# Window attention and routed experts on one core: grouped one-hots, split first loads, and weights loaded at other steps

## The chip, the core and the metric

The kernel runs on one NeuronCore of a Trainium2 chip. A core has five engines that run side by side, each taking its own instructions in order: TensorE (PE in the profile; PEld is its loading of weights, which overlaps the multiplying), VectorE (DVE), ScalarE (ACT), GpSimd (POOL) and SyncE (SP, which here only issues transfers). SBUF is the working memory of 128 partitions, PSUM the eight banks into which PE writes its products. Transfers between DRAM and SBUF run on 16 DMA engines that all issuing engines share.

The metric is the time of one execution in microseconds of the device, lower is better. The kernel before took 696.98 us, the median of three runs (695.01, 696.98, 697.22).

## The reference, cut to what matters

Two blocks follow each other. The first is attention of 8 batches x 8 heads over 576 positions of width 64, where a position sees itself and the 63 before it. Its output, regarded as 4608 tokens of width 512, goes through a layer of eight experts of which each token uses one.

```python
scores = scale * np.matmul(q, k.transpose(0, 1, 3, 2))
mask = (rel >= 0) & (rel < 64)              # rel = query position - key position
scores = np.where(mask, scores, -1e9)
attn = np.exp(scores - scores.max(-1, keepdims=True))
attn = attn / (attn.sum(-1, keepdims=True) + 1e-9)
x = np.matmul(attn, v)                      # then (B, H, S, D) -> (4608, 512)

logits = x @ w_gate                         # 8 experts
expert_idx = np.argmax(logits, axis=1)
gate_w = ...                                # the softmax probability of that expert
h = np.maximum(x_of_expert @ w1[e], 0.0)    # w1[e]: 512 x 1024
y_of_expert = h @ w2[e]                     # w2[e]: 1024 x 512
out = gate_w[:, None] * y                   # each row back in its token's place
```

All numbers are float32.

## The kernel before

**Attention.** A *unit* is two batches (a group, `BG = 2`) and two heads (a head pair, `g`); there are 16 units. Each has nine tiles of 128 queries, taken three at a time: a *step*, 48 in all. Eight tiles come from the first 512 positions of the two batches, the ninth from their last 64 positions (the *ends*, "rests" in the code, which are loaded for all eight heads of a group at once by `load_rests`).

The order of instructions is written out by hand: `step(s)` emits for several steps at once what keeps PE busy. In one call PE gets, in this order, `scored(s+1)` (scores, L700), `weighted(s-1)` (attention times v, L746), at the end of a unit the logits of its three steps (L783), `flipped(s)` (transposes of the exponentials, L731, copied to SBUF at L733), `turned(s+3)` (transposes of q and k that step s+3 needs, L665 and L657, copied at L670 and L660) and `x_turned(s-2)` (L771). DVE masks scores and takes their extremes (`masked`, L713) and divides by the sums (L756 to L760); ACT takes the exponentials (L723). Two banks hold scores, so the scores of a step wait for the masking of the step before. The calls begin at s = -3, so that `turned(0)` comes first; the call for s = -2 leaves its `turned` out, and the call for s = -1 makes up for it, after `scored(0)`.

Loads for later units are issued at the first step of a unit, on SP: the ends if a new group is near, then v two units ahead, then q and k three units ahead (`load_qk`, L614). v is kept in two forms. `load_v` loads the first (L637), and POOL copies it shifted by 64 positions into the second (L638, L642, L646), directly behind the issue. So POOL's later work stands in its queue behind the landing of that v.

Other work hangs in `todo[s]`, a list that is emitted at the end of step s: the loading of the first expert's w1 (four pieces on ACT's queue at steps 1, 2, 4 and 5), the four sums of its quarters on POOL (`left_sums`, steps 9 to 12), the routing of a finished group (`choose`), and the weighting of its rows by the gate with their storing in `x_dram` (`weigh` on POOL, L886; `store`).

**Routing and the table of slots.** Tokens of an expert get consecutive places, in tiles of 256 tokens. The table `perm_i` that says which token sits in which slot is made by matmuls: the slot's number splits into a high part (the column) and a low part (the partition). `lo` holds a one-hot of the low part, `hi` one of the high part, and a token's number is brought in as two bf16 factors, `toks`, so that it stays exact. Before, `lo` holds both planes, each already multiplied by one of the factors, made by `place(j)` one column of tokens after the other (two DVE instructions per column, L875), and the table is the sum of 72 matmuls (L927). A first, small table for expert 0's first two tiles is made before the last group is routed (`first_tiles`, L982 and L990, 54 matmuls).

**Experts.** A product of a whole tile is seven quarter products (Strassen's scheme in Winograd's form): `hidden` makes seven products with w1's quarters and their sums (L353), `output` seven with w2's (L397). `tile0` and `tile1` are expert 0's first two tiles. Both are generators: each `next` emits one product and what belongs to it, so that other work can be put between. `tile0` is emitted between pieces of the last group's routing and of `slot_table`. Tokens of the following tile are fetched from `x_dram` by `gather` (POOL, L285), and turned by 16 block transposes on DVE (`turned_blocks`, L324); in `tile1` all 16 stand in `output`, behind the sums of h (L142), and in front of ACT's copies (`keep_turned`, L336). The tile behind is a half tile (L453). `load_w1(1)` and `load_w2(1)` (L159, L162) are emitted on SP after `tile1`; their memory is the attention's, so they wait until the table's matmuls have read `hi`.

**Start.** POOL makes the mask by eleven selections over pieces of it (L587 to L590), DVE clears four columns of `lo` (L998), and PE runs eight matmuls on them while the first q and k are under way (L1000). The ends of group 0 are issued directly behind unit 0's q and k.

The few lines that place the work around the change:

```python
if s + 3 < N and s != -2:
    if s == -1:
        turned(1)
    turned(s + 3)
...
xsp = held.enter_context(tc.tile_pool(name="xsp", bufs=7))
...
tile1 = chain(hidden(0), output(0, blocks))
```

## Time and profile before

| | before |
|---|---|
| median of three runs | 696.98 us |
| the profiled execution's own time | 692.44 us |
| its span, first to last instruction | 690.7 us |
| granted TensorE clock | 0.997 |
| busy: PE, PEld | 671.8 us (97%), 590.5 us (85%) |
| busy: DVE, ACT, POOL | 500.6, 262.2, 357.0 us |
| moved by DMA | 94.51 MB in 135742 packets |
| packets under 512 bytes | 114543 |

The page counts an engine as busy while one of its instructions runs. Matmuls are pipelined and their ends are modelled, so short waits of PE are read better from PEld, whose records follow each other at a fixed distance while PE is supplied. In a row of the timeline stand the start in us, the busy us, engine, line, operation, what is written from what, the form and the number of instructions; a bracket at its end gives the engine's idle time before the row and what ended it. The name of a releaser is inferred, and can be wrong where several waits end together. The stages are: attention to about 189 us, `tile0` with the last routing and the table to 232, `tile1` to 257, and then the tiles of all experts.

### The profile page before, as it was taken

Reading aid. Unit: us, or ns where it says so; the run is one execution under the profiler, and the core shown is the slowest. Engines: PE = TensorE matmul, PEld = TensorE weight load, DVE = VectorE, ACT = ScalarE, POOL = GpSimd, SP = SyncE. Lnnn points to the kernel's source line nnn. Section 1 sums busy time; section 2 is a strip of 40 time slices with the busy share of each in tenths; the row PEclk is TensorE's granted clock in tenths of the full one; section 3 lists DMA queues with packets and bytes.
Section 4 is the critical chain, followed back from the end, with each engine's and each line's share of the span. In section 5 each row is a group of like instructions: output and inputs, shape, how many; then the busy total and the mean of one; then the engine's idle time right before and its main releaser. Section 6 shows DMA issues by size and latency. Waiting matters only on the chain. (4 is left out here: it accounts for less than half of the span.)

```text
span 690.7 us, 17952 instructions
## 1 busy us (share of the span) xinstructions
PE 671.8 (97%) x6902; PEld 590.5 (85%) x6902; DVE 500.6 (72%) x1650; ACT 262.2 (38%) x660; POOL 357.0 (52%) x364
## 2 busy tenths in 40 slices
PE   7999999999999999999999999999899999999996
PEld 5888888888788987998899899899599799689995
DVE  5767898898959578775686586577767586866864
ACT  4989888889845011211121121111121121121211
POOL 7316578577771218676451446446265756264012
PEclk9999999999999999999999999999999999999998
DMA  9999888877524442723601171270145171211012
GB/s 216 251 210 199 192 206 244 202 199 198 162 78 168 155 157 77 268 69 128 230 1 64 61 262 44 70 269 32 65 156 190 51 256 51 65 39 63 2 63 61
DMA packets 135742, 94.51 MB, mean 137 GB/s; under 512 B 114543, under 2 KB 114559, under 8 KB 135616
## 3 DMA queue, kind: packets, MB, share of 16 engines
q1 hardware_dynamic: 113952, 38.28, 22.4%
q0 software_dynamic: 8544, 26.50, 11.9%
q10 hardware_dynamic: 13120, 28.05, 11.3%
q8 instruction: 78, 1.28, 0.7%
q14 instruction: 48, 0.39, 0.2%
HBM read 73.94 MB, written 20.45 MB: 137 GB/s over the span
## 5 line engine op out<-in xcount | busy, mean ns | idle before, releaser
L324 DVE STREAM_TRANSPOSE v_m<-qk_m 32x256 f32<-32x256 f32 x320 | 139.3, 435 | 6.8 <-DMA qk_m<-x_dram,at_g 0.8
L285 POOL DMA_INDIRECT qk_m<-x_dram,at_g x42 | 45.1, 1075 | 164.2 <-DVE v_m L324 154.1
L353 PE MATMUL bank<-qk_m,s 128*128 128x128 f32 x1024 | 122.5, 275 | 0.0
L353 PEld LDWEIGHTS bank<-qk_m,s 128*128 128x128 f32 x1024 | 118.3, 192 | 0.0
L723 ACT ACTIVATE pr<-pr,mx 128x128 f32<-128x128 f32 x288 | 89.6, 391 | 22.2 <-DVE mx L713 21.7
L353 PE MATMUL bank<-qk_m,w 128*128 128x128 f32 x768 | 94.2, 276 | 1.0 <-PEq L1166 0.6
L353 PEld LDWEIGHTS bank<-qk_m,w 128*128 128x128 f32 x768 | 90.3, 192 | 4.6 <-issue 4.3
L713 DVE CUSTOM_DVE_ANT_0 pr<-bank,mask 128x128 f32<-128x128 f32 x288 | 64.4, 286 | 15.8 <-PE bank L700 14.6
L304 POOL DMA_INDIRECT out_dram<-v_m,at_s x42 | 42.5, 1011 | 56.9 <-DVE v_m L393 52.7
L393 DVE TENSOR_TENSOR v_m<-bank,v_m 128x256 f32<-128x256 f32 (+1 forms) x95 | 43.8, 480 | 38.1 <-PE bank L397 27.3
L142 POOL TENSOR_TENSOR s<-w 128x1024 f32<-128x1024 f32 x22 | 52.2, 2374 | 0.0
L638 POOL COPY v_m<-v_m 64x520 f32<-64x520 f32 x32 | 19.8, 618 | 62.1 <-DMA v_m<-in_v_dram 52.8
L397 PE MATMUL bank<-qkT_m,v_m 128*128 128x256 f32 x216 | 48.3, 379 | 0.0
L746 PEld LDWEIGHTS bank<-v_m,pT 128*64 128x64 f32 x1152 | 40.4, 137 | 9.0 <-issue 3.4
L746 PE MATMUL bank<-v_m,pT 128*64 128x65 f32 x1152 | 47.4, 227 | 0.1
L360 ACT COPY qk_m<-bank 128x512 f32<-128x512 f32 x16 | 9.4, 587 | 99.9 <-PE bank L353 73.7
L336 ACT COPY qk_m<-v_m 128x512 f32<-128x512 f32 x40 | 22.7, 615 | 61.4 <-DVE v_m L324 61.4
L397 PEld LDWEIGHTS bank<-qkT_m,v_m 128*128 128x128 f32 x216 | 41.0, 190 | 5.5
L700 PE MATMUL bank<-qkT_m 64*64 64x128 f32 x1152 | 43.1, 278 | 1.6 <-DVE qkT_m L670 1.6
L886 POOL TENSOR_SCALAR xs<-xs,gate 128x512 f32<-128x512 f32 x27 | 42.2, 1574 | 0.9 <-DVE gate L846 0.3
L731 PE MATMUL bank<-ident,pr 128*128 128x128 f32 x288 | 42.0, 282 | 0.0
L363 DVE TENSOR_TENSOR qk_m<-bank,qk_m 128x512 f32<-128x512 f32 x16 | 11.1, 692 | 40.7 <-PE bank L353 40.7
(202 smaller groups left out, 1249.2 us busy)
## 6 DMA issues: line engine op xcount, KB each, us to landing
w<-in_moe_w_dram ACTq DMA_DIRECT2D x9, 2048.0 KB, 8.1
qk_m<-in_q_dram SPq DMA_DIRECT2D x32, 256.0 KB, 5.1
v_m<-in_v_dram SPq DMA_DIRECT2D x64, 128.0 KB, 4.3
qk_m<-in_k_dram SPq DMA_DIRECT2D x30, 256.0 KB, 5.1
qk_m<-in_moe_w_dram ACTq DMA_DIRECT2D x3, 2048.0 KB, 10.6
w<-in_moe_w_dram SPq DMA_DIRECT2D x2, 2048.0 KB, 14.2
w<-in_moe_w_dram ACTq DMA_DIRECT2D x4, 512.0 KB, 5.8
x_dram<-xs POOLq DMA_DIRECT2D x4, 512.0 KB, 5.6
```

The lines of the kernel that those rows point to most:

```text
L142: op()
L285: G.indirect_dma_start(out=xg[c], out_offset=None, in_=x_dram[:, :], in_offset=bass.IndirectOffsetOnAxis(ap=at_g[:, c : c + 1], axis=0),)
L304: put = G.indirect_dma_start(out=out[:, :], out_offset=bass.IndirectOffsetOnAxis(ap=at_s[:, c : c + 1], axis=0), in_=ys[c], in_offset=None ...
L324: V.transpose(out=xn[b * QD : (b + 1) * QD, :, :, a * QD : (a + 1) * QD].rearrange("p c g i -> p (c g) i"), in_=rows[a * QD : (a + 1) * QD ...
L353: nc.tensor.matmul(acc[:, f, :], lhsT=a[:, g, f * P : (f + 1) * P], rhs=b[:, g, :], start=(first and f == 0 and g == 0), stop=(g == HG - 1 ...
L393: plus = lambda out, a, b: V.tensor_tensor(out=out, in0=a, in1=b, op=ALU.add)
L397: nc.tensor.matmul(acc, lhsT=a[:, f, :], rhs=b[:, f, :], start=(start and f == 0), stop=(stop and f == HF - 1), skip_group_check=True,)
L700: nc.tensor.matmul(out_, lhsT=qT[rows, t, a * WINDOW : (a + 1) * WINDOW], rhs=rhs, start=True, stop=True, skip_group_check=True,)
L713: V.tensor_tensor_reduce(out=prs[h][:, m, :], in0=scs[h][:, m, :], in1=mask[:, m0 + m, :], scale=-scale, scalar=-2 * MASKED, op0=ALU.add, ...
L723: nc.scalar.activation(out=y, in_=y, func=AF.Exp, scale=-1.0, bias=mx[:, h, m : m + 1])
L746: nc.tensor.matmul(px[a * D : (a + 1) * D, h, m, :], lhsT=pTs[h][:, m, a * D : (a + 1) * D], rhs=vt[:, h, :], start=True, stop=True, skip_ ...
L886: engine.tensor_scalar(out=y, in0=y, scalar1=s, scalar2=None, op0=ALU.mult)
```

## The change

It has six parts.

1. *One-hots.* `lo` keeps one plane of pure one-hots, made for three columns of tokens by one DVE instruction. The token numbers move to the other factor: `with_tokens` multiplies `hi` by the first factor on POOL and by the second, which no longer depends on the column, on ACT. `table_of` makes a table with half as many matmuls, each with twice the columns; all 36 stand after the last piece of `tile0`.
2. *Copies of v.* `copy_v` is separate from `load_v` and is emitted one step later, ahead of that step's other work.
3. *Ends by head pairs.* The ends of group 0 are loaded for the first two heads ahead of unit 1, and for the other six behind unit 1's q and k, k now on SP.
4. *Start.* The mask takes three selections and three DVE copies; `lo` is cleared before everything else; `turned(1)` stands before `scored(0)`, and the copies of q at steps 0 and 1 are ACT's, those of k DVE's.
5. *First w1.* Its four pieces are issued at steps 15, 17, 19 and 21, its sums made at steps 27 to 30.
6. *Tile 1.* Twelve of the 16 block transposes stand in `hidden`, four after each of its fourth, fifth and sixth products; the memory of the attention is given back before `tile1`, and expert 1's w1 and w2 are loaded on ACT's queue after its third and fifth products.

The buffers for rows of x go from seven to eight.

```diff
+    lo = consts.tile([P, NJ, P], BF16, name="lo")
+    nc.vector.memset(lo[:, 0:4], 0.0)
...
-    def hidden(e, blocks=iter(())):
+    def hidden(e, blocks=iter(()), shares=(6, 2, 2, 2)):
...
-        some(blocks, 6)
+        some(blocks, shares[0])
...
-        for h in range(2):
-            for m0, m1, first in ((0, 1, False), (1, 2, h == 0), (2, NM, False)):
...
+        half = mask[0:D]
+        nc.gpsimd.memset(half[:, 1:3], 0.0)
+        sel(1, -1, ALU.is_ge, 0)
+        sel(2, 1, ALU.is_gt, 0)
+        sel(2, -1, ALU.is_ge, WINDOW)
+        nc.vector.tensor_copy(out=half[:, 0], in_=half[:, 2])
+        nc.vector.tensor_copy(out=half[:, 3:NM], in_=_ins(half[:, 2], 1, NM - 3))
+        nc.vector.tensor_copy(out=mask[D:P], in_=_ins(half[:, 2], 1, NM))
...
-                (nc.vector.tensor_copy if s + n > 0 and s < BG else nc.scalar.copy)(
+                (nc.vector.tensor_copy if n and s < BG else nc.scalar.copy)(
...
         def place(j):
-            for i in range(2):
-                V.tensor_scalar(
-                    out=lo[:, i, j], in0=lane[:], scalar1=low[:, j : j + 1], scalar2=toks[i][:, j : j + 1],
-                    op0=ALU.is_equal, op1=ALU.mult,
-                )
+            js = slice(j, j + ST)
+            V.tensor_tensor(out=lo[:, js], in0=_inner(low[:, js], P), in1=_ins(lane[:], 1, ST), op=ALU.is_equal)
+
+        def with_tokens(hi, js):
+            n, ns = js.stop - js.start, hi.shape[3]
+            G.tensor_tensor(out=hi[:, 1, js], in0=hi[:, 0, js], in1=_inner(tok_a[:, js], ns), op=ALU.mult)
+            nc.scalar.activation(
+                out=hi[:, 2, js].rearrange("p j s -> p (j s)"), in_=hi[:, 0, js].rearrange("p j s -> p (j s)"),
+                func=AF.Copy, scale=tok_b[:],
+            )
+
+        def table_of(perm, hi, n, bank, first):
+            slots = bank(0, 2, hi.shape[3])
+            for j in range(n):
+                nc.tensor.matmul(slots, lhsT=lo[:, j], rhs=hi[:, 1:, j], start=(j == 0), stop=(j == n - 1))
+            V.tensor_scalar_add(first, slots[:, 0], float(NT))
+            V.tensor_tensor(out=perm, in0=slots[:, 1], in1=first, op=ALU.add)
...
-        load_rests(0)
+        load_rests(0, slice(0, 2), nc.scalar)
         load_qk(1, (0,))
         load_v(0)
         load_qk(1, (1,))
+        load_rests(0, slice(2, H))
         load_v(1)
+        copy_v(0)
+        copy_v(1)
         load_qk(2)
...
-            step = NST * (g // 2) + g % 2 + 1
+            step = 5 * NST + 2 * g
...
-            todo.setdefault(3 * NST + n, []).append(op)
+            todo.setdefault(9 * NST + n, []).append(op)
...
                     load_v(u + 2)
+                    todo.setdefault(s + 1, []).insert(0, partial(copy_v, u + 2))
...
-            if s + 3 < N and s != -2:
-                if s == -1:
-                    turned(1)
+            if s + 3 < N:
                 turned(s + 3)
...
-        tile1 = chain(hidden(0), output(0, blocks))
-        for _ in range(8):
+        held.close()
...
+        tile1 = chain(hidden(0, blocks, (0, 4, 4, 4)), output(0, blocks))
+        for n in range(8):
             next(tile1)
+            if n in (2, 4):
+                (load_w1 if n == 2 else load_w2)(1, nc.scalar)
...
-        load_w1(1)
-        load_w2(1)
```

## The prediction

> **What bounds the kernel now.** I read the page's engine shares and slices first, then a table of busy time by stage, then the timeline of TensorE (PE) alone wherever that table is not full.
>
> ```profile
> PE 671.8 (97%) x6902; PEld 590.5 (85%) x6902; DVE 500.6 (72%) x1650; ACT 262.2 (38%) x660; POOL 357.0 (52%) x364
> ...
> DMA  9999888877524442723601171270145171211012
> ```
>
> PE is busy for 97% of the span, and the transfers fill the DMA engines in the first ten slices (173 us). Columns below: stretch, length, then busy us (instructions) of PE, PEld, DVE, ACT, POOL, the granted clock, the DMA share, GB/s.
>
> ```profile
> 0.00:16.00 16.00, 12.39 (x137) 8.47 (x137) 8.45 (x52) 7.33 (x20) 11.90 (x38) 1.00 1.02 220
> 16.00:28.50 12.50, 12.41 (x207) 10.76 (x205) 9.80 (x58) 11.98 (x37) 3.43 (x8) 1.00 0.95 246
> 28.50:52.60 24.10, 23.18 (x419) 19.71 (x418) 16.34 (x97) 20.55 (x59) 6.24 (x13) 1.00 0.93 221
> 52.60:63.90 11.30, 11.30 (x212) 9.88 (x211) 8.18 (x49) 10.15 (x30) 5.17 (x12) 1.00 0.87 193
> ...
> 189.20:256.90 67.70, 65.80 (x640) 58.99 (x639) 46.90 (x147) 22.35 (x48) 19.50 (x17) 1.00 0.42 144
> 256.90:690.70 433.80, 423.94 (x3084) 377.09 (x3084) 299.96 (x635) 80.24 (x152) 221.67 (x175) 1.00 0.31 105
> ```
>
> A unit (three steps) whose PE never waits takes 11.3 us (52.6 to 63.9). So time is to be had only at the start (3.6 us of PE missing in 16), between 28.5 and 52.6 (24.1 us for two units), and in 189 to 257. After 257 the change touches nothing but what it shifts. The start, on PE:
>
> ```profile
> 5.36 1.92 PE L665 MATMUL bank<-ident,qk_m 128*128 128x128 f32 x8
> 8.15 0.89 PE L700 MATMUL bank<-qkT_m 64*64 64x128 f32 x24 [0.88 <-DVE qkT_m L670]
> 11.81 0.67 PE L700 MATMUL bank<-qkT_m 64*64 64x128 f32 x16 [0.76 <-DVE qkT_m L670]
> 12.40 0.87 PE L731 MATMUL bank<-ident,pr 128*128 128x128 f32 x6
> 17.95 0.45 PE L700 MATMUL bank<-qkT_m 64*64 64x128 f32 x8
> ```
>
> Scores of step 1 wait at 11.81 for copies of transposed q and k that VectorE (DVE) makes only after masking step 0. Two units on, PE waits for q and k themselves:
>
> ```profile
> 39.45 0.63 PE L665 MATMUL bank<-ident,qk_m 128*128 128x128 f32 x4 [0.36 <-DMA qk_m<-in_k_dram]
> 47.13 0.63 PE L665 MATMUL bank<-ident,qk_m 128*128 128x128 f32 x4 [0.36 <-ACT pr L723]
> 47.97 0.63 PE L665 MATMUL bank<-ident,qk_m 128*128 128x128 f32 x4 [0.21 <-DMA qk_m<-in_k_dram]
> ```
>
> The DMA records give k landings of 39.31 and 47.83 and a q landing of 47.00 here, so all three are transfers that came just in time, whatever releaser is named. The table and the tile after it:
>
> ```profile
> 223.91 1.14 PEld L927 LDWEIGHTS <-lo 128*128 128x128 bf16 x37 [0.70 <-DVE qk_m L342]
> 225.47 0.56 PEld L927 LDWEIGHTS <-lo 128*128 128x128 bf16 x17 [0.42 <-issue]
> 231.03 0.78 PEld L927 LDWEIGHTS <-lo 128*128 128x128 bf16 x18
> ...
> 256.94 1.11 PEld L453 LDWEIGHTS bank<-qk_m,w 128*128 128x128 f32 x8 [0.73 <-issue]
> ```
>
> PE stands before the table for two DVE results, and at 256.94 for transposed tokens that DVE finishes at 255.66 and ScalarE (ACT) copies by 256.8.
>
> **The start (-1.7 us).** *Warm-up:* the zeroing of lo moves from 1.65 to DVE's first instruction, 0.88, so the eight matmuls of 0.427 us end near 4.6 instead of 5.4. The first q half landed at 4.43, k at 5.22; those transposes then end near 6.1, not 6.9. *Order:* turned(1) now stands before scored(0). Its data landed at 6.57 and 7.08, its eight transposes take 0.109 us each at the pitch of 8.97 to 10.06, so scored(0) starts near 7.6 (was 8.15) and masking near 8.65 (9.20). scored(1) then needs only the two banks that masking frees, six times 0.21 us later: 10.0, ending 10.9, so masking 1 starts at 10.95 instead of 12.53. The following order is unchanged, ACT is continuously busy from there (12.86 to 21.2) and shifts with it: scored(3) at 16.2 instead of 17.95. *Mask:* eight fewer selections of 0.29 to 0.53 us on POOL, whose mask then ends near 5 instead of 7.86; three DVE copies replace them, and DVE is idle until 7.31. No cost; without that cover about 1 us. *Queues:* on SP the q and k ends are split, 32 KB each in front, 96 KB behind unit 1, four more issues of about 0.65 us on SP (two of them were ACT's) and two of 0.75 us on POOL; the same bytes, 384 KB of them no longer ahead of unit 1. Bounds: 0, if k of batch 1 lands no earlier than scored(0) ran, to -2.5, if masking 1 also finds cold transposes gone (0.85 us for eight at 0.2135).
>
> **Just-in-time transfers (-1.6 us).** The first w1, four pieces of 512 KB, was issued at 18.06, 21.13, 28.60 and 32.57. Units 2 to 4 landed 0.1 to 0.5 us before use then. At 215 GB/s, 2 MB is 9.8 us of transfer that leaves this stretch, more than the 1.7 us by which PE comes earlier. The PEld waits at 38.7, 46.4 and 47.4 (0.60, 0.57, 0.42) go; a next lateness would be unit 2 (landed 23.2, used 23.8). Bounds -1.6 to 0. Later copy_v frees POOL of waits (52.8 us in all for v), but no PE wait names a v copy: 0.
>
> **The w1 at steps 15 to 21 (0).** Four ACT issues of 0.35 us move. There unit 7 landed 11.8 us before use, unit 8 10.0, so 9.8 us is covered, narrowly; see the rivals. The four sums of 2.37 us on POOL move from 64-77 to steps 27 to 30, again beside routing; the unit at 64 took 12.14 us, so about 0.75 us of DVE contention moves, not goes: 0, bounds -0.4 to +0.8. One-hots: six DVE instructions 0.223 us apart become one of about 0.56 (L919's 1.32 us for 1116 elements and L982's 0.27 for 108 give 1.04 ns an element). That is 0.8 us of DVE for each of 12 groups, on no path that ends a PE wait: 0, at best -0.8.
>
> **First tiles (-0.7).** 54 matmuls of 28 ns (1.5 us) become 27. The multiplications wait for hi_e: POOL 108 elements, ACT 108, about 0.4 us, after a DVE that gets there 0.8 us sooner; weighted(45) keeps PE until then. perm_e needs one more DVE instruction (0.17). The gather behind it moves with PE, so its 0.52 us wait at 199.16 stays. Bounds -0.9 to +0.4, should both engines answer late.
>
> **Slot table (-1.2).** Matmul columns stay (72 x 62 = 36 x 124): at 28 ns for 62, 2.0 us either way. All now stand behind output(0), so the waits of 0.70 and 0.42 go. New: POOL multiplies 1116 elements twice, 2.37 us per 1024, so 2.6 each, from 222.8 and 225.5 to 228.2; PE reaches the first matmul that needs the second half near 229.4. ACT needs 1.1 us each beside 14 us of idleness. So covered by 1.2 us; bounds +1.0 (POOL late by its own length less the cover) to -2.2 (36 matmuls at the 28 ns pitch).
>
> The row says POOL stood still for 22.7 us just there. The Trainium skill, "GPSIMD Engine Reference", section "When to use GPSIMD", is against it: two-input elementwise work belongs on VectorE, GpSimd being about half as fast. Counted on the path, as that rule would, the two multiplications would turn the sum of -5.9 into -0.7; I go by the idle time.
>
> **Tile 1 (-0.7).** Twelve of sixteen transposes (7.17 us for all) move from behind hidden(0) between its DVE operations, 1.8 us per group. They need the gather, which lands 3.7 us after issue (median), near 237, since the 4 MB of weights that delayed it to 242.9 now start near 236.7 and 242 on ACT. DVE's chain u3, 4, hq11, 4, hq10, 4, hq01, relu, two sums gives hs1 at 248.0; PE wants it at 248.2. The last four end near 251, well ahead of 254.9, so the 0.73 us goes. w2 lands near 252, first read by POOL after 262. Bounds -0.8 to +0.5.
>
> **Sum.** -1.7 -1.6 -0.7 -1.2 -0.7 = -5.9 us. The profiled execution took 692.44 (span 690.7, 1.74 around it): 686.5. The median shown is 696.98, 0.7% above it, so 691.1; I say 691.0. Below 0.3% (2.1 us) a measurement of this kernel tells nothing.
>
> **Rivals.** *The early queue still decides:* q, k, v in 256-byte pieces filled the engines (share 0.93 to 1.02) also in slices with no w1; then the first two terms shrink from -3.3 to -1: 693.4. *Tile 1 starves:* if the gather lands at 240.98/242.87 as before, each us after 238.5 delays hs1 by one, 4.4 us in all: of the sum without its own term, 5.2, 0.8 is left: 696.2, no change. For it: transposes sit in front of hq11 in DVE's queue; against: nothing large is in flight at 233. *The moved w1 blocks q, k, v (slower):* its pieces took 4.1 to 6.4 us to land, 22 us together. If SP's transfers stood still for all of it, unit 7 would come 22 - 11.8 = 10 us late: 701. It decides against the change beyond 18 us of standstill. Against: 338 GB/s moved in 20 to 25 us with two pieces in flight, so both queues ran. *One part does nothing:* a table that waits on POOL as long as it did on DVE: 692.3.
>
> **How the numbers follow.** Forecast 0.60 (687.5 to 693.5), early queue 0.15, table 0.07, tile 1 starves 0.08, w1 blocks 0.07, neutral for other reasons 0.03. Faster is the first three, 0.82, within 0.3% the starved tile and the neutral, 0.11, slower 0.07. Range 686.8 to 696.2, which leaves out the slow case and the tail below.
>
> **What would show it.** After: L700 for step 3 near 16.2; no PE wait on L665 before 60; the one table stretch of 36 matmuls without a DVE wait; L453 of tile 1 without one. Wrong if PE waits on L665 between 75 and 100, on POOL at the table, or on DVE near 248.

## The result and the profile after

The changed kernel took 695.11 us, the median of 14 runs (693.44 to 698.55), and the kernel before 695.15 in 14 runs of its own. The ratio is 1.0009, with a 95% interval of 0.999 to 1.0028: no difference that this measurement can tell. The profiled execution of the changed kernel took 694.31 us (span 692.5), that of the one before 692.44 (span 690.7), so the two traces differ by 1.8 us. Line numbers have moved: scores L700 are L711 now, the transposes of q and k L665 are L676, those of the exponentials L731 are L742, attention times v L746 is L757, x_turned L771 is L782, the products of an expert L353 and L397 are L358 and L402, the half tile L453 is L458.

The page of the changed kernel, first its row of TensorE and then the DMA share in 40 slices:

```profile
PE 672.6 (97%) x6839; PEld 592.8 (86%) x6839; DVE 496.0 (72%) x1595; ACT 266.5 (38%) x664; POOL 359.1 (52%) x361
...
DMA  9999799969443272542701172171146171111012
```

The table by stage of the changed kernel, with the columns of before (stretch, length, busy us of PE, PEld, DVE, ACT, POOL, granted clock, DMA share, GB/s):

```profile
0.00:16.00 16.00, 12.87 (x80) 8.21 (x81) 6.96 (x42) 5.48 (x14) 8.92 (x31) 1.00 1.11 180
16.00:28.50 12.50, 12.50 (x226) 10.94 (x226) 8.73 (x53) 11.93 (x36) 4.14 (x9) 1.00 1.09 201
28.50:52.60 24.10, 24.10 (x445) 21.18 (x443) 17.83 (x109) 21.70 (x63) 8.18 (x17) 1.00 1.00 199
...
87.40:189.20 101.80, 95.48 (x1698) 82.13 (x1696) 86.52 (x441) 85.44 (x246) 81.37 (x92) 0.98 0.90 211
189.20:256.90 67.70, 65.89 (x674) 59.23 (x667) 48.88 (x157) 29.17 (x66) 25.76 (x21) 1.00 0.47 156
256.90:692.50 435.60, 426.95 (x3106) 380.70 (x3104) 299.62 (x636) 81.45 (x154) 221.97 (x175) 1.00 0.31 105
```

The stretch from 28.5 to 52.6, in which PE missed 0.9 us, is full now. But in the first 16 us PE issues 80 instructions where it issued 137, while the transfers fall from 220 to 180 GB/s; and between 87 and 189 it has a hole: PE misses 6.3 us there (2.2 before), at a mean granted clock of 0.98. The time from mark to mark, each mark being PE's first weight load of the work named (from the two traces; a step is named by its scores), tells what each stretch gained:

| stretch | before | after | change | predicted |
|---|---|---|---|---|
| span's start to step 3 | 17.94 | 20.70 | +2.76 | -1.7 |
| step 3 to step 15 | 45.93 | 44.39 | -1.54 | -1.6 |
| step 15 to step 29 | 54.57 | 53.55 | -1.02 | 0 |
| step 29 to step 35 | 23.06 | 29.36 | +6.30 | 0 |
| step 35 to step 47 | 47.70 | 47.22 | -0.48 | 0 |
| step 47 to tile 0's first product | 11.18 | 10.47 | -0.71 | -0.7 |
| tile 0's first product to tile 1's | 31.37 | 30.19 | -1.18 | -1.2 |
| tile 1's first product to the half tile | 25.19 | 25.24 | +0.05 | -0.7 |
| half tile to the end | 433.79 | 431.38 | -2.41 | 0 |
| sum | 690.73 | 692.50 | +1.77 | -5.9 |

Three terms came as worked out, to 0.1 us. Two stretches lost 9.1 us that the prediction had as -1.7 and 0, one gained nothing, and one gained 2.4 that nobody had counted on. The two losses, in the timeline of the changed kernel. First the start, PE alone:

```profile
5.71 1.94 PE L676 MATMUL bank<-ident,qk_m 128*128 128x128 f32 x8 [0.86 <-DMA qk_m<-in_q_dram]
8.46 1.97 PE L676 MATMUL bank<-ident,qk_m 128*128 128x128 f32 x8 [0.81 <-DMA qk_m<-in_q_dram]
10.36 1.56 PE L711 MATMUL bank<-qkT_m 64*64 64x128 f32 x24
...
12.74 2.18 PE L711 MATMUL bank<-qkT_m 64*64 64x128 f32 x24 [0.21 <-DVE mx L724]
...
17.31 0.89 PE L711 MATMUL bank<-qkT_m 64*64 64x128 f32 x24
```

PE waits for q twice. Batch 1's q landed at 8.42 (6.57 before). The 24 matmuls of step 0 and step 1 then take 1.56 and 2.18 us instead of 0.89, so the matmuls there run at about half speed. The records of the granted clock begin only at 16.5 us in this trace; in that of the kernel with the later sums (below) the clock is 0.50 from 8.9 to 12.3 us, and there, too, step 0 takes 1.56 us. Then the hole:

```profile
131.82 2.36 POOL L1066 TENSOR_TENSOR s<-s,w 128x1024 f32<-128x1024 f32 x1
131.94 2.27 DVE L867 TENSOR_TENSOR count<-count,r_inc 128x8 f32<-128x8 f32 x1
...
134.14 2.42 POOL L1066 TENSOR_TENSOR s<-w 128x1024 f32<-128x1024 f32 x1
134.39 2.26 DVE L872 TENSOR_TENSOR r_rank<-r_rank,r_ranks 128x72 f32<-128x72 f32 x1
...
138.44 0.55 PE L782 MATMUL bank<-ident,xs 128*128 128x128 f32 x3 [3.72 <-DVE pT L744]
138.91 1.17 PE L711 MATMUL bank<-qkT_m 64*64 64x128 f32 x24
140.02 1.62 PE L757 MATMUL bank<-v_m,pT 128*64 128x65 f32 x24
```

L1066 are the moved sums of w1. A DVE addition of eight numbers per partition, 0.17 us in the other three groups' routing, begins 0.1 us after a sum and ends when it ends. The next long one does the same, 0.25 us after its sum began, and a third, L835 at 123.0, took 2.39 us (0.23 elsewhere). DVE's copies for PE queue behind them. The hole costs more than its length: from 139.4 to 142.8 us the granted clock is 0.50, and the three groups of matmuls from 138.91 to 142.93 take 4.02 us, which take 2.50 at 65.10. So some 1.5 of the 6.3 us are slow matmuls behind the hole.

### The profile page after: what moved, and what is told of

Its sections match the earlier page's. It is cut to its first block, busy times and chain, and to the rows that moved or that the text cites. A ratio compares the mean times of both kernels' runs of the same rounds, so it can differ in the third digit from the quotient of the medians.

```text
span 692.5 us, 17772 instructions
## 1 busy us (share of the span) xinstructions
PE 672.6 (97%) x6839; PEld 592.8 (86%) x6839; DVE 496.0 (72%) x1595; ACT 266.5 (38%) x664; POOL 359.1 (52%) x361
## 5 line engine op out<-in xcount | busy, mean ns | idle before, releaser
L358 PE MATMUL bank<-qk_m,s 128*128 128x128 f32 x1024 | 122.4, 275 | 0.0
L358 PEld LDWEIGHTS bank<-qk_m,s 128*128 128x128 f32 x1024 | 118.3, 192 | 0.0
L358 PE MATMUL bank<-qk_m,w 128*128 128x128 f32 x768 | 94.1, 276 | 0.8 <-PEq L1177 0.6
L358 PEld LDWEIGHTS bank<-qk_m,w 128*128 128x128 f32 x768 | 90.3, 192 | 4.4 <-issue 4.1
L757 PEld LDWEIGHTS bank<-v_m,pT 128*64 128x64 f32 x1152 | 40.8, 139 | 9.5 <-issue 3.3
L757 PE MATMUL bank<-v_m,pT 128*64 128x65 f32 x1152 | 47.6, 229 | 0.8 <-DVE pT L744 0.7
L402 PE MATMUL bank<-qkT_m,v_m 128*128 128x256 f32 x216 | 48.1, 379 | 0.0
L402 PEld LDWEIGHTS bank<-qkT_m,v_m 128*128 128x128 f32 x216 | 41.0, 190 | 5.6
L711 PE MATMUL bank<-qkT_m 64*64 64x128 f32 x1152 | 44.8, 285 | 0.2 <-DVE mx L724 0.2
L742 PE MATMUL bank<-ident,pr 128*128 128x128 f32 x288 | 42.6, 285 | 0.0
```

Source lines behind the costliest of these rows:

```text
L358: nc.tensor.matmul(acc[:, f, :], lhsT=a[:, g, f * P : (f + 1) * P], rhs=b[:, g, :], start=(first and f == 0 and g == 0), stop=(g == HG - 1 ...
L402: nc.tensor.matmul(acc, lhsT=a[:, f, :], rhs=b[:, f, :], start=(start and f == 0), stop=(stop and f == HF - 1), skip_group_check=True,)
L711: nc.tensor.matmul(out_, lhsT=qT[rows, t, a * WINDOW : (a + 1) * WINDOW], rhs=rhs, start=True, stop=True, skip_group_check=True,)
L742: nc.tensor.transpose(out=tr[:, m, :], in_=prs[h][:, m, :], identity=ident[:])
L757: nc.tensor.matmul(px[a * D : (a + 1) * D, h, m, :], lhsT=pTs[h][:, m, a * D : (a + 1) * D], rhs=vt[:, h, :], start=True, stop=True, skip_ ...
```

## The experiments

Each is compared with the kernel before on the same chip. Traces are single executions, and those of the later kernels lie at the upper end of their timed runs; so a stretch is read from a trace, a verdict from the runs.

### The hole: sums on POOL against the routing on DVE

**Sums later** (the changed kernel):

```diff
-            todo.setdefault(9 * NST + n, []).append(op)
+            todo.setdefault((33, 33, 35, 37)[n], []).append(op)
```

> The changed kernel with one edit: the four sums of the first w1 on POOL move from steps 27 to 30 to steps 33, 33, 35 and 37. Theory A (a DVE operation whose two sources both lie in SBUF and that begins inside one of these POOL sums lasts until the sum ends: 2.39, 2.27 and 2.26 us for operations of 0.23, 0.17 and 0.23): at steps 33 to 37 DVE has only a one-hot operation of 0.55 us now and then, so the step starts 29 to 35, 6.3 us later against before in the changed kernel's trace, fall back to the pace of before. About 6 us less than the changed kernel: some 689 where that is at 695. Rival B (w1 or the other moved transfers hold the routing up): no change, 695. If the sums hit the one-hot operations instead, 1 to 4 us less only.

695.34 us against 693.14, a ratio of 1.0031 (1.0007 to 1.0055): no gain. The trace shows why. The hole is gone: steps 30 to 35 take 19.5 us (25.3 in the changed kernel, 19.2 before). But the time comes back elsewhere, in the trace's stretch from step 47 to tile 0, 16.05 us instead of 10.47:

```profile
187.45 4.64 POOL L911 TENSOR_SCALAR xs<-xs,gate 128x512 f32<-128x512 f32 x3
...
198.59 1.16 POOL L299 DMA_INDIRECT qk_m<-x_dram,perm_e  x1 [5.27 <-DVE xs L771]
...
202.34 0.63 PE L320 MATMUL bank<-ident,qk_m 128*128 128x128 f32 x4 [3.66 <-DMA qk_m<-x_dram,perm_e]
```

Four sums of 2.4 us among the gate multiplications of group 1 make POOL late for those of group 2: they end at 192.1, although PE scores step 47 5.6 us earlier than in the changed kernel, where they ended at 190.3. Rows are stored and gathered only behind them, and PE waits for the gather. So theory A held for its stretch and failed for the total: POOL's time there is not free. One of the sums also met a grouped one-hot of DVE, which took 2.57 us (0.55 alone); steps 36 to 39 became 0.6 us longer than in the changed kernel.

**Sums at 27 to 30 in the kernel before**, w1 as early as ever:

```diff
-            todo.setdefault(3 * NST + n, []).append(op)
+            todo.setdefault(9 * NST + n, []).append(op)
```

> The kernel before with one edit: the four sums of the first w1 move to steps 27 to 30, and w1 is loaded as early as before. Theory A (the sums on POOL hold the routing's DVE operations): 4 to 6 us slower than before, with DVE operations of L856 to L861, 0.17 to 0.23 us elsewhere, lasting over 2 us, and PE waiting 3 to 4 us behind them. Rival B (the moved loads do it): as before, within 1 us.

697.49 us against 693.14, ratio 1.0071 (1.0044 to 1.0097), by which it is 4.9 us slower. Steps 30 to 35 lose 5.3 us, without any moved transfer:

```profile
125.77 1.43 DVE L845 TENSOR_SCALAR gate<-gate 128x9 f32<-128x9 f32 x1
...
129.58 2.36 POOL L1053 TENSOR_TENSOR s<-w 128x1024 f32<-128x1024 f32 x1
129.93 2.17 DVE L851 TENSOR_TENSOR_SCAN r_inc<-keep,r_ranks 128x72 f32<-128x72 f32 x1
...
135.39 0.55 PE L771 MATMUL bank<-ident,xs 128*128 128x128 f32 x3 [2.26 <-DVE pT L733]
```

Here it was above all the scan L851 (0.30 us elsewhere) that took 2.17 us, to the end of that sum, and not the lines I had named. Theory A, that the sums hold the routing, is shown, and rival B is out. The Trainium skill has the rule behind these rows, "SBUF — State Buffer", section "Who interferes with whom": a DVE instruction with two SBUF inputs contends with a GpSimd instruction that reads SBUF, and the one that comes second waits for the whole of the other. The rows of 2.17 to 2.39 us agree; so does the masking, one of whose inputs is a PSUM bank and which stayed at 0.28 us inside a sum (136.52 us in the changed kernel). But two sources are not the whole condition: L845 adds a constant to nine numbers, one source, and took 1.43 us inside a sum (0.17 elsewhere).

**w1 at 15 to 21 and sums at 33 to 37 in the kernel before:**

```diff
-            step = NST * (g // 2) + g % 2 + 1
+            step = 5 * NST + 2 * g
...
-            todo.setdefault(3 * NST + n, []).append(op)
+            todo.setdefault((33, 33, 35, 37)[n], []).append(op)
```

> The kernel before with w1 loaded at steps 15, 17, 19 and 21, and its four sums at steps 33, 33, 35 and 37. The prediction's term for just-in-time transfers: PE's waits at 38.7, 46.4 and 47.4 go, 1.6 us; and steps 15 to 29 gain what the changed kernel gained there, 1.0 us, if that too comes from the sums and the loads and not from the grouped one-hots. So 1.6 to 2.6 us faster than before. If the changed kernel's gain there came from its own late start (its units had more time to land), nothing: within 0.5 us. If w1 blocks q, k and v: PE waits for them from step 18 to 30, slower.

694.14 us against 693.14 (1.0015, 1.0002 to 1.0029). Up to step 21 the trace gains 2.3 us against before, and q and k of units 3 and 4 land 6.1 to 7.6 us before use (0.1 to 1.6 before): the just-in-time term is there. Then it is lost, 3.9 us between steps 36 and 39, where two of the sums held one-hots of DVE, the old form with one source tensor, for 1.65 and 2.35 us (0.30 alone), and 1.3 before tile 0. The forecast gain of 1.6 to 2.6 us did not come.

**w1 at 4 to 10, sums at 12 and 13** (the changed kernel):

```diff
-            step = 5 * NST + 2 * g
+            step = 4 + 2 * g
...
-            todo.setdefault(9 * NST + n, []).append(op)
+            todo.setdefault(12 + n // 2, []).append(op)
```

> The changed kernel with w1 loaded at steps 4, 6, 8 and 10 and its sums on POOL at steps 12, 12, 13 and 13, where POOL stands idle in every trace so far and DVE has no operation on two SBUF sources. Theory A with its second half (the sums hold DVE in the routing at 27 to 30; at 33 to 37 they hold POOL, whose gate multiplications then end 2 us later and delay the first gather): the 6 us of steps 29 to 35 go and nothing comes in their place: 688.5 to 690 where the changed kernel takes 695 and the one before 695, that is 0.992 of before. Rival B (the time comes back elsewhere, as with sums at 33 to 37, by q and k late beside w1 or a late gather): 0.998 to 1.003 of before.

690.23 us against 695.45, ratio 0.9924 (0.9897 to 0.9951): the hole is gone and nothing of its size takes its place. One sum still met the first routing, whose L835 took 1.94 us at 77.6.

### The start

**The old mask** (the changed kernel with the eleven selections of before):

```diff
-        half = mask[0:D]
-        nc.gpsimd.memset(half[:, 1:3], 0.0)
...
+        nc.gpsimd.memset(mask[:], 0.0)
+        for h in range(2):
...
```

> The changed kernel with the mask of before (twelve selections and a memset on POOL), so that POOL issues the gate's and the v ends' transfers some 3.7 us later again. Theory S1 (these small transfers, brought forward by the short mask, slowed q and k of batch 1): q of batch 1 lands near 6.6 to 7.1 instead of 8.4, and step 3 scores near 18 to 19 instead of 20.7. Rival S2 (the order, transposes of batch 1 in front of the scores of step 0, makes step 0 wait) and rival S3 (the warm-up ends at 4.85 and leaves TensorE idle and slow): step 3 still at 20 to 21.

A single run, 698.43 us (the selections are eleven, not twelve). POOL's transfers were issued at 7.87 us again, and q of batch 1 still landed at 8.3, so theory S1 is out. Step 3 scored at 18.97, inside S1's forecast, but for another reason: here the matmuls of step 0 took 0.89 us, not 1.56.

**The ends whole**, and then **the old order** (each the changed kernel):

```diff
-        load_rests(0, slice(0, 2), nc.scalar)
+        load_rests(0, slice(0, H), nc.scalar)
...
-        load_rests(0, slice(2, H))
```

> The changed kernel with one edit: the ends of q, k and v of the first batch group are loaded whole again, all eight heads at once, ahead of unit 1 (k by ACT, v by POOL), as before; order, mask and warm-up stay changed. Theory R (the ends split by heads slow all transfers: 218 instead of 288 GB/s from 4.5 us on in three profiles of kernels with the split, 288 up to 10 us in three without): q of batch 1 lands at 6.2 to 6.6 instead of 8.3 to 8.4, step 0 scores at 7.6 to 8.2 and step 3 at 16.2 to 17.5, which is the prediction's first term. Rival S2 (the new order alone costs the time): step 3 still at 19 to 20.7. Rival S3 (warm-up ends too early): transfers fast, but matmuls of step 0 at half speed, step 3 at 18 to 19.

```diff
-            if s + 3 < N:
-                turned(s + 3)
+            if s + 3 < N and s != -2:
+                if s == -1:
+                    turned(1)
+                turned(s + 3)
```

> The changed kernel with one edit: the transposes of batch 1 stand behind the scores of step 0 again. Theory R: q of batch 1 still lands near 8.4, but step 0 scores at about 8.5 without waiting for it; step 1 waits instead; step 3 at 19 to 20, little gained. Rival S2: step 3 at 18 as before.

Single runs, 693.92 and 692.38 us. Step 3 scored at 21.64 and at 21.16, later than in the changed kernel, and q of batch 1 landed at 7.7 and 7.5 (6.57 before). Theory R and rival S2 fall: no single part of the visible start makes the transfers slow. A third kernel, with whole ends, w1 at steps 4 to 10 and the sums at 12 and 13, says the same of theory R:

> Both edits: the ends loaded whole and the early w1 and sums. If both theories hold, the two gains add: the start gives 3 to 4 us against the changed kernel, the sums 6: 685 to 686.5 where before takes 695, a ratio of 0.985 to 0.988. If q and k, no longer relieved by the split ends and beside an early w1, come just in time again at 38 to 48 us, 1.5 us less of it: 0.989. If the gain of the start is given back at the next wait: 0.992, as with the sums alone.

690.46 us, ratio 0.9929 (0.9902 to 0.9955), as without the whole ends. All of these kernels had one thing in common that I had not looked at. The rate of the DMA engines from 1 to 10 us in 40 slices, of before, then of the changed kernel:

```profile
GB/s 0 0 0 0 0 0 94 35 205 206 247 256 280 287 289 291 285 290 290 289 291 282 290 287 288 287 284 290 287 285 286 289 285 288 291 288 287 288 288 290
```

```profile
GB/s 0 0 0 0 0 6 100 212 173 129 283 288 285 291 289 257 219 218 220 217 220 217 215 215 220 216 216 218 207 220 155 174 84 155 174 191 227 230 222 255
```

From 4.6 to 7.8 us it is 207 to 220 instead of 282 to 291, with the engines just as full. The pieces are the same, 256 bytes each, but one takes 26 ns on average (4.6 to 7 us) instead of 18. What changed is where they go: `lo` and the token tiles lie in front of the tile `qk_m` in SBUF and became shorter, so that it starts at byte 64,576 and no longer at 73,984. The old start is a multiple of 256, the new one 64 past one.

**The tile at a multiple of 256** (the changed kernel), and **64 bytes past one** (the kernel before):

```diff
+    consts.tile([P, 48], F32, name="pad")
     qk_m = Memory(consts.tile([P, 10240], F32, name="qk_m"))
```

> The changed kernel with one edit: 192 unused bytes stand in front of the tile that takes q and k, so that it starts at byte 64768 of SBUF, a multiple of 256, and no longer at 64576, 64 past one. Before the change it started at 73984, a multiple of 256; the shorter one-hot and token tiles moved it. Theory T (a start that is no multiple of 256 slows transfers made of 256-byte pieces: 218 GB/s instead of 288 between 5 and 10 us, in all six traces of kernels with the changed tiles, whatever the order, the mask and the ends): 285 to 290 GB/s until 10 us, q of batch 1 lands at 6.2 to 6.6, step 3 scores at 16 to 17 instead of 20.7, so 3 to 4 us off the start, and 691.5 to 692.5 in all. Rival (the earlier end of the warm-up, or the pattern of the queues, does it): 218 GB/s and step 3 at 19 to 20.7 still.

```diff
+    consts.tile([P, 16], F32, name="pad")
     qk_m = Memory(consts.tile([P, 10240], F32, name="qk_m"))
```

> The kernel before with one edit: 64 unused bytes in front of the same tile, which then starts 64 bytes past a multiple of 256. Theory T: 215 to 240 GB/s between 5 and 10 us instead of 288, q of batch 1 at 7.3 to 8.4 instead of 6.2 to 6.6, step 3 at 19 to 21, and 2 to 4 us slower as a whole. Rival: no difference, step 3 at 17.7 to 18.3.

The changed kernel with 192 unused bytes took 691.04 us against 694.0, a ratio of 0.9956 (0.9936 to 0.9977); the kernel before with 64 took 700.09, 1.0079 (1.0049 to 1.0109). Their rates, the aligned one first:

```profile
GB/s 0 0 0 0 0 5 90 231 224 241 240 252 280 291 290 284 289 289 289 288 289 288 289 279 288 259 256 285 291 303 296 267 291 291 304 260 361 242 244 252
```

```profile
GB/s 0 0 0 0 0 6 150 167 35 154 218 290 289 289 285 287 248 220 221 216 220 213 221 217 218 220 216 219 215 215 206 179 173 184 165 175 201 174 181 183
```

And PE's scores of steps 0 and 3 in the aligned kernel:

```profile
8.18 0.89 PE L712 MATMUL bank<-qkT_m 64*64 64x128 f32 x24
...
16.59 0.89 PE L712 MATMUL bank<-qkT_m 64*64 64x128 f32 x24
```

Step 3 scores at 16.59, 4.1 us earlier than in the changed kernel and 1.35 earlier than before; in the shifted one at 21.75. This settles the start: what cost it is the shift of the tile, a side effect of the shorter tiles in front, and not the order, the mask or the split ends. S3 is out too, since the aligned kernel keeps the early warm-up and runs step 0 in 0.89 us. The Trainium skill has a rule that points the same way, "DMA: Bandwidth & Descriptors", section "How a descriptor splits into AXI transactions": for a piece that does not start at a multiple of 256 bytes the first transaction starts at the boundary below, and the unused bytes still cost beats. By its count a 256-byte piece 64 past one takes 10 beats instead of 8, an estimate of 230 GB/s from 288; measured were 213 to 221. The count does not explain all of the trace: until 4.4 us the pieces took 18 ns in the shifted kernels too, and from 20 to 40 us the mean was 20.8 ns in the changed kernel (18.2 before). The unused bytes also move the tiles behind `qk_m`; but between 5 and 7 us no load of v had been issued in either shifted kernel (the first at 7.3 and 8.7), so nearly all pieces under way then are for `qk_m`.

### Both mended, and what is left

**Tile aligned, w1 at steps 4 to 10, all four sums at step 11:**

```diff
+    consts.tile([P, 48], F32, name="pad")
...
-            step = 5 * NST + 2 * g
+            step = 4 + 2 * g
...
-            todo.setdefault(9 * NST + n, []).append(op)
+            todo.setdefault(11, []).append(op)
```

> The changed kernel with the tile of q and k at a multiple of 256 bytes, w1 loaded at steps 4, 6, 8 and 10 and its four sums on POOL at step 11, ahead of the copies of v that wait for their transfer. Theories A and T together: the start as with the aligned tile alone (3 to 4 us), no long DVE operation in either routing (6 us against the changed kernel, and 1.5 to 2 us more than sums at steps 12 and 13, one of which still held a DVE operation of the first routing for 1.94 us): 684.5 to 686.5 where before takes 695, a ratio of 0.985 to 0.988. If the tile changes nothing: 688 to 689, 0.990.

686.57 us against 694.0, ratio 0.9893 (0.9867 to 0.992). After step 3 PE waits at most once on q or k, 0.31 us at 23.1. But the sums ran behind v copies that waited for their transfer, and met the first routing:

```profile
70.81 2.37 POOL L1067 TENSOR_TENSOR s<-w,s 128x1024 f32<-128x1024 f32 x1
70.99 2.28 DVE L831 TENSOR_TENSOR r_top<-r_top,e_m 128x72 f32<-128x72 f32 x1
...
75.37 0.55 PE L783 MATMUL bank<-ident,xs 128*128 128x128 f32 x3 [2.43 <-DVE pT L745]
```

**w1 where it was before, or a little later** (aligned; at the steps of before with the sums at 9 to 12, and at 2, 4, 6, 8 with the sums at 9, 9, 11, 11):

```diff
-            step = 5 * NST + 2 * g
+            step = NST * (g // 2) + g % 2 + 1
...
-            todo.setdefault(9 * NST + n, []).append(op)
+            todo.setdefault(3 * NST + n, []).append(op)
```

> The changed kernel with the tile at a multiple of 256 bytes, and with w1 loaded and summed at the steps of before (1, 2, 4, 5 and 9 to 12). If the moved loads were needed for the just-in-time term, PE waits for k again between 38 and 48 us, some 1.5 us, and step 15 scores at 63 to 63.5 instead of 62.0. If the waits of before were chance of that execution, or the ends behind unit 1 relieve them: none, step 15 at 62.0 to 62.3. The sums meet the first routing once (0.5 to 2 us at steps 15 to 21).

```diff
-            step = 5 * NST + 2 * g
+            step = 2 + 2 * g
...
-            todo.setdefault(9 * NST + n, []).append(op)
+            todo.setdefault(9 if n < 2 else 11, []).append(op)
```

> The changed kernel with the tile of q and k at a multiple of 256 bytes, w1 loaded at steps 2, 4, 6 and 8, and its sums at steps 9, 9, 11 and 11: POOL stands idle there from 53 to 60 us and from 63 to 69, and the first routing begins at 70. Theories A and T: no DVE operation over 2 us, step 21 scores at 85 instead of 88.7, step 47 at 186.5; about 3.5 us less than with the four sums at step 11, a ratio of 0.984 to 0.986 to before. That is -10 us, more than the predicted -5.9, since the grouped one-hots gave 1.0 and the loss of 0.5 to the sums of before goes too. If something else takes its place: 0.989 as with step 11.

688.2 and 688.61 us against 693.51, ratios 0.9914 (0.9884 to 0.9944) and 0.9915 (0.9881 to 0.9948). No sum meets a routing, and PE waits for q and k instead. PE in the one with w1 as before:

```profile
24.48 0.63 PE L677 MATMUL bank<-ident,qk_m 128*128 128x128 f32 x4 [2.03 <-DMA qk_m<-in_q_dram]
26.59 1.09 PE L677 MATMUL bank<-ident,qk_m 128*128 128x128 f32 x4 [1.48 <-DMA qk_m<-in_k_dram]
```

and with w1 at 2 to 8:

```profile
48.18 0.63 PE L677 MATMUL bank<-ident,qk_m 128*128 128x128 f32 x4 [1.52 <-DMA qk_m<-in_q_dram]
50.25 0.63 PE L677 MATMUL bank<-ident,qk_m 128*128 128x128 f32 x4 [1.44 <-DMA qk_m<-in_k_dram]
```

So an early w1 does cost 3 us of waits, at places other than those of before, and more behind them: the granted clock was 0.50 from 26.3 to 29.7 and from 50.7 to 54.2 us, and the three steps with the waits took 15.9 and 16.2 us (steps 3 to 6 and 9 to 12; 10.5 and 11.3 in the changed kernel). It is not always so: the kernel before with only the sums moved had no such wait between 18 and 75 us.

**Tile 1.** The changed kernel with its 16 block transposes in one piece again:

```diff
-        tile1 = chain(hidden(0, blocks, (0, 4, 4, 4)), output(0, blocks))
+        tile1 = chain(hidden(0), output(0, blocks))
```

> The changed kernel with the sixteen block transposes of the tile after the table in one piece again behind the hidden layer, as before; its weights are still loaded by ACT behind the gathers. The prediction had -0.7 for the interleaved transposes; the traces show from the tile's first product to the half tile 25.24 us after and 25.19 before, the 0.73 us wait of before gone and a new one of 0.86 us in its place, behind ACT's copy of an output bank that queues behind the last relu. If the two cancel for that reason: no wait in the output, 0.7 us before the half tile again, 25.2 us. If the gathers, landing later, cost it: the wait before the half tile grows to 1 us and more, 25.5 to 26 us.

A single run, 694.36 us: tile 1 takes 25.20 us, the same, with no wait in the output and 0.73 us ahead of the half tile, as before. In the changed kernel the wait before the half tile is gone, but PE waits in the output:

```profile
250.93 0.69 DVE L389 TENSOR_TENSOR qk_m<-bank,qk_m 128x512 f32<-128x512 f32 x1
251.65 0.63 ACT L390 ACTIVATE qk_m<-qk_m 128x512 f32<-128x512 f32 x1 [1.90 <-DVE qk_m L389]
252.19 0.35 ACT L416 COPY v_m<-bank 128x256 f32<-128x256 f32 x1
...
252.60 1.99 PE L402 MATMUL bank<-qk_m 128*128 128x256 f32 x8 [0.48 <-ACT v_m L416]
```

The third product of the output adds to a bank that ACT must have copied, and that copy stands behind a relu whose DVE input came late by the transposes. The kernel above with w1 at 2 to 8, and shares of two:

```diff
-        tile1 = chain(hidden(0, blocks, (0, 4, 4, 4)), output(0, blocks))
+        tile1 = chain(hidden(0, blocks, (0, 2, 2, 2)), output(0, blocks))
```

> The same, and the transposes of the tile after the table by two behind three steps of the hidden layer and ten behind its last sums, instead of four, four, four and four. Theory: ACT's copy of the first output bank waits behind a relu that waits for DVE, and DVE was held by 5.3 us of transposes in its chain; with 2.7 us the copy comes in time, the wait of 0.86 us goes, and the ten transposes end some 4 us before the half tile wants them: tile 1 takes 24.4 us instead of 25.2, a ratio 0.001 below the other. Rival: the ten come too late and the half tile waits: 25.2 us or more.

```profile
247.57 0.37 ACT L417 COPY v_m<-bank 128x256 f32<-128x256 f32 x1 [0.38 <-PE bank L403]
249.10 1.89 PE L403 MATMUL bank<-qk_m 128*128 128x256 f32 x8
249.88 4.49 DVE L330 STREAM_TRANSPOSE v_m<-qk_m 32x256 f32<-32x256 f32 x10
```

The copy comes in time, both waits are gone, and tile 1 takes 24.48 us, 0.71 less than before. The total, 687.7 us (0.9904, 0.9869 to 0.9939), can't resolve so little.

**The best version:** tile aligned, w1 at 4, 6, 8 and 9 (the sums at step 9 already read the last piece), sums at 9, 9, 11 and 11, shares of two.

```diff
+    consts.tile([P, 48], F32, name="pad")
...
-            step = 5 * NST + 2 * g
+            step = min(4 + 2 * g, 9)
...
-            todo.setdefault(9 * NST + n, []).append(op)
+            todo.setdefault(9 if n < 2 else 11, []).append(op)
...
-        tile1 = chain(hidden(0, blocks, (0, 4, 4, 4)), output(0, blocks))
+        tile1 = chain(hidden(0, blocks, (0, 2, 2, 2)), output(0, blocks))
```

> The changed kernel with the tile of q and k at a multiple of 256 bytes, w1 loaded at steps 4, 6, 8 and 9, its sums at steps 9, 9, 11 and 11, and the transposes of the tile after the table by two, two, two and ten. If loads that start at step 4 leave q and k in time (as 4, 6, 8, 10 did with the sums at step 11) and the sums run at 55 to 60 and 64 to 69 us, ahead of the first routing at 70: no PE wait on q or k after 20 us, step 21 scores at 85, step 47 at 186.5, tile 1 takes 24.5 us; 3.6 and 0.7 us less than with the sums at step 11: a ratio of 0.982 to 0.984 to before. If q and k come late again, between 44 and 51 us as with w1 at 2 to 8: 0.989 to 0.991.

684.92 us against 693.2, ratio 0.9879 (0.9845 to 0.9912): 8.3 us faster than before. Of the waits above only 1.07 us at 23 to 24 us and 0.6 in the first routing are left. Expected was 0.982 to 0.984, just below the interval.

## Why the prediction was wrong

The time, 695.11, lies inside the range given only because that range reaches up past the kernel before (695.15). The forecast was a gain of 5.9 us, and none came; without the 2.4 us that came by luck behind the half tile the kernel would have become slower. (The 696.98 that the sum starts from was itself 1.8 us above the median of fourteen runs.)

- **The start (-1.7, bounds 0 to -2.5): measured +2.8.** The step that failed is "the same bytes". I had counted bytes, pieces and issues of each queue and not the addresses: the shortened tiles moved `qk_m` off its multiple of 256, and from 4.6 to 18 us most pieces took 22 ns and more instead of 18. Most of the working held once the tile was aligned: step 3 scores at 16.59 there (16.2 foretold, -1.35 instead of -1.7). In the six traces with the aligned tile it is 16.6 to 17.9, in the three of the old start without the shift 17.7 to 18.3. The rival "the early queue still decides" had the right place and a smaller price: it made the terms shrink, not turn.
- **Just-in-time transfers (-1.6): measured -1.54,** and full PE from 28.5 to 52.6. That moving w1 gives it is supported by the slack in b_w1_later and by the 3 us of waits that came back with an early w1. The size is chance in part, since one trace with an early w1 had none of these waits.
- **w1 at 15 to 21 (0): right.** PE does not wait for q or k between 75 and 100. The rival that the moved w1 blocks q, k and v did not occur.
- **Sums at 27 to 30 (0, bounds -0.4 to +0.8): measured +6.3.** This is the step that lost the gain. I had taken the sums for 0.75 us of contention wherever they stand. In fact each can hold a DVE operation that meets it for up to 2.4 us, and PE's wait behind them is followed by slow matmuls (1.5 of the 6.3). At their old place, 64 to 77 us, they met one such operation, L824, near the end of a sum (0.51 us); at the new place they fell on the routing, which is made of such operations in a chain.
- **Grouped one-hots (0, at best -0.8): measured -0.97,** 0.48 in each of the first two groups (steps 21 to 24 and 36 to 39). Steps 36 to 39 take 11.3 us in thirteen of the fourteen traces with the grouped one-hots and 11.8 or more in the four with the old ones. So they do stand on a path that ends PE waits, if only for a little. Another 0.45 in steps 15 to 21 is the place that the sums left.
- **First tiles (-0.7): -0.71. Slot table (-1.2): -1.18.** Neither is chance of one trace: step 47 to tile 0 takes 10.4 to 10.6 us in thirteen of the fourteen traces with the changed code (11.0 to 12.5 in the four with the old), and tile 0 to tile 1 30.2 to 30.3 (31.4). The term went by POOL's idle time, which was there before:

```profile
232.26 0.18 POOL L283 COPY at_g<-perm_i 128x2 int32<-128x2 int32 x1 [22.74 <-DVE perm_i L937]
```

  POOL's second multiplication ended 0.12 us into the table, before the matmuls that need it; it was covered, as worked out:

```profile
231.56 2.31 POOL L891 TENSOR_TENSOR hi<-hi,tok_a 128x1116 bf16<-128x1116 bf16 x1 [1.26 <-DVE hi L944]
```

```profile
233.75 2.17 PEld L901 LDWEIGHTS <-lo 128*128 128x128 bf16 x36
```

- **Tile 1 (-0.7): +0.05.** The gathers landed by 243.4 and did not starve it. I had followed DVE's chain to hs1 and missed ACT's queue, in which the copy of an output bank stands behind the last relu.
- **After the half tile (0): -2.4,** luck, as no part of the change aims at it; see the last section.

## What to carry to other kernels

When a change resizes any tile, look up where the tiles behind it now start, before pricing anything else: here 64 bytes made the kernel 0.8% slower, and 192 unused bytes in front mended it; other offsets were not measured. When work moves on POOL, list the DVE operations that will run beside it by their operands: those with sources in SBUF, two above all, can be held until the POOL instruction ends, so long two-input POOL work goes beside masking from PSUM, not beside chains of small operations. And time on POOL that a trace shows idle is only free at that place; the same 9.5 us were free at 55 to 69 us and cost a late gather at 143 to 171.

## What I had not expected of the hardware

- Transfers of 256-byte pieces from 4.8 to 6.6 us: 279 to 291 GB/s to a tile at a multiple of 256 bytes, 213 to 221 to one 64 past it, with either code. From 3.7 to 4.4 us they ran at 280 to 291 in either. Why the loss sets in only near 4.6 us and is mostly gone behind 20 us is open, and so is how other offsets fare.
- A wait of TensorE can cost more than its length, and need not. Behind the 3.72 us in the changed kernel the granted clock was 0.50 for 3.4 us; behind 0.95 us at 182 us in the kernel before, 24 matmuls took 0.89 as ever. At the start it goes both ways. In the changed kernel it waited 0.86 and 0.81 us, and step 0's 24 matmuls took 1.56 us; in the one with the old mask it waited 1.06 and 0.53 us, and they took 0.89.
- Before, PE stops twice inside L500, near 493 and 600 us, for nothing that the profile names. The first, and then the same place in the changed kernel:

```profile
491.07 1.93 PE L500 MATMUL bank<-w,qk_m 128*32 128x256 f32 x30
494.39 4.20 PE L500 MATMUL bank<-w,qk_m 128*32 128x256 f32 x18 [1.39 <-issue]
```

```profile
495.33 5.52 PE L505 MATMUL bank<-w,qk_m 128*32 128x256 f32 x48 [0.29 <-issue]
```

  All four traces with the old routing code have these two stops, 1.7 to 2.0 and 1.1 to 1.3 us between the starts of two weight loads; none of the fourteen with the changed one has them. They make up the 2.4 us after the half tile and more. An instruction transfer of 16 KB ran from 491.7 to 492.9, as the first stop began; in the changed kernel one ran from 496.5 to 497.4, inside the same line, and PE did not stop. With 63 matmuls fewer in front, PE's code may lie elsewhere in its pieces; that this is the cause is not shown.
